# GpSimd's sums of the second weights (experts 3 to 7) in six operations of 128x384 in place of three of 128x768

## The chip, the cores and the metric

The kernel runs on one core of one Trainium2 chip. Its time is the device time of one execution in microseconds (us), lower is better. Five engines of the core take part, each with its own queue of instructions in order: PE (TensorE, the matrix products), DVE (VectorE), ACT (ScalarE), POOL (GpSimd) and SP (SyncE, which issues most DMAs). PEld is the loading of the stationary operand on PE; it overlaps the products. Everything here is float32.

## The reference, cut to what matters

An attention-like recurrence makes 3072 rows of 384 numbers. Each row then goes to the one of eight experts with the highest gate value, through two matrices of that expert with a ReLU between them:

```python
y = _attn_ref(q, k, v, f_logit)          # state = f * state + k v^T ; y = q . state
x = y.transpose(0, 2, 1, 3).reshape(B * S, H * D)     # 3072 x 384
logits = x @ w_gate                                   # 384 x 8
expert_idx = np.argmax(logits, axis=1)
...
for e in range(E):                                    # 8 experts
    h = np.maximum(x_sorted[lo:hi] @ w1[e], 0.0)      # w1: 384 x 1024
    y_sorted[lo:hi] = h @ w2[e]                       # w2: 1024 x 384
...
return gate_w[:, None] * y
```

## The kernel before, in words

The first third of the program is the recurrence, the routing and a scatter of the rows into one region of DRAM per expert. The change touches only what follows: a loop over the experts, with three tiles of 128 rows (or 352 rows, where short leftovers ride along) for each.

**The wide part of an expert** is x @ w1. It is not done as a plain product but by a fast scheme over blocks, with fewer products and more sums: `w1` is cut into 4 x 3 blocks (256 hidden columns by 128 inputs each) and the rows into halves. 17 sums and differences of the blocks of `w1`, each 128x256, are made ahead (lines 1302 to 1307, tiles `was` and `w1t`; "the first sums" from here on); DVE makes sums of the rows (`xbs`). `widen_sums` then runs 20 products on PE, two matmuls each, into five PSUM banks. Their results are put together by a table of steps, `WIDE_STEPS`: `keep` is a copy of a bank to SBUF by ACT (line 1415), `join` an addition of a bank and an SBUF tile by DVE, `more` an addition of two SBUF tiles by DVE (both line 1392), `rect` a ReLU by ACT (line 1422). A new product that needs a bank waits for the last reader of that bank. The steps that the prediction speaks of stand in this order in the table:

```
add:c31:a32:bs4 join:c31:c31:+:c10
more:c31:c31:-:c11 rect:c31:- add:t4:a30:bs6 keep:t4:h0 pass:t4:t1 ...
new:t9:as3:bs7 keep:t9:c20 pass:t9:c11 join:c11:c11:+:c01
more:c11:c11:+:c10 rect:c11:+ ... join:c01:c01:+:c00 ...
```

In ACT's queue the order is: ReLU of `c31`, then the copy `h0` (tile `hold`, which frees the bank of `t4` for the product `as5`), then the copy of `t9`. In DVE's queue: join and `more` of `c31`, two joins, `more` of `c11`, the join of `c01` (which frees a bank for the product with `a22`).

**The narrow part** is h @ w2. The last tile of 128 rows goes through a plain product (`narrow_riding` or `narrow_late`). The other two tiles go as a pair (`narrow_pair`) through a scheme with seven products of half blocks in place of eight. It needs three sums of quarters of `w2`, made by `weight_sums`: `t1`, `t2`, `t4`, each 128 x 4 x 192, which is 768 numbers per partition ("the second sums", line 1298, tiles `wsum1`, `wsum2`, `wsum4`). `t2` reads `t1`, and `t4` reads `t2`. For experts 0 to 2 DVE makes them, for experts 3 to 7 POOL.

**The order of the work** is written out by hand: each engine runs its instructions in the order of the code, under `manual_schedule`. For an expert e above 2 the code gives POOL this: the second sums of e, the first sums of e+1, the scatter of the riding tile's rows of e, the two scatters of the pair of e (line 260; the pair's two wait for DVE's `ysb`, line 1480), then the second sums of e+1, and so on. PE runs the wide part of e, the last tile, the pair of e, the wide part of e+1; between them stand short products for leftover rows (lines 1256 and 1279). So POOL begins the second sums of an expert at about the time at which PE begins that expert's wide part.

Of the kernel before, what the change touches and what calls it, by code (L numbers as in the profile page):

```python
# [170 lines left out]
def kernel(  # L171
# [15 lines left out]
    nc = tc.nc  # L187
# [189 lines left out]
    def load_rows(row, count=C):  # L377

        rows = xs[ds(row, count)] if not isinstance(row, int) else xs[row : row + count]
        n, whole = -(-count // C), count // C  # L380
        wholes = rowp.tile([128, TILES * C // BK, DB], F32, name="xrow")
        x = wholes[:, 0 : count // BK]
        tg = rowp.tile([128, TILES, USED - TOK], F32, name="tg", bufs=4)[:, 0:n]
        reads = load_blocks(x, rows)
        reads.append(
            nc.sync.dma_start(
                tg[:, 0:whole], rows[0 : whole * C, TOK:USED].rearrange("(t p) r -> p t r", p=C)
            ).ins
        )
        if n > whole:  # L390
            nc.sync.dma_start(tg[0 : count - whole * C, whole], rows[whole * C :, TOK:USED])
        return {"n": n, "rows": count, "x": x, "tg": tg, "reads": reads, "whole": wholes}
# [821 lines left out]
    with ExitStack() as st:  # L1214
# [80 lines left out]
        HB = NF // 2  # L1295

        def minus(to, a, b, on=nc.vector):
            on.tensor_tensor(to, a, b, op=OP.subtract)  # L1298
# [125 lines left out]
        def weight_sums(w, on=nc.vector, room=None):  # L1424

            b = [
                [w[1][:, HB * i : HB * i + HB, HD * j : HD * j + HD] for j in range(2)]
                for i in range(2)
            ]
            if room is None:  # L1430
                t1, t2, t4 = (qp.tile([128, HB, HD], F32, name=f"wsum{i}") for i in (1, 2, 4))
            else:
                t1, t2, t4 = (
                    room[:, 2 * i : 2 * i + 2].rearrange("p a (b d) -> p (a b) d", b=2)
                    for i in range(3)
                )
            minus(t1, b[0][1], b[0][0], on)
            minus(t2, b[1][1], t1, on)
            minus(t4, b[1][0], t2, on)
            return b, t1, t2, t4  # L1440

        def hidden_parts(x):
# [98 lines left out]

        rooms = [qp.tile([128, NF, DM], F32, name="qw2", bufs=4) for i in range(3)]
        made = {0: weight_sums(weights[0])}
        turn(rows_of[0])
        made[1] = weight_sums(weights[1], room=rooms[0])

        def tasks(e, hook):
# [24 lines left out]
        def wide_part(e):  # L1572
            x, w = rows_of[e], weights[e]
            x["wide"] = e not in PLAIN
            if e == 1:
                x["hT"] = rooms[2][:, :, 0 : x["rows"]]
            else:
                x["hT"] = qp.tile([128, NF, TILES * C], F32, name="hT")[:, :, 0 : x["rows"]]
            wide_quad(3 * e)
            tasks(e, 0)  # L1580
            fetch(3 * e)
            if e > 1:
                made[e] = weight_sums(w, nc.vector if e == 2 else nc.gpsimd)
            if e + 1 < E and e != 1:
                prepare_weights(rows_of[e + 1], weights[e + 1])
            if x["wide"]:
                widen_sums(x)
            else:
                widen(x, w, bank, range(NF))
            if e > 0:  # L1590
                nc.scalar.copy(x["dst"], x["tg"][:, :, 0])
# [31 lines left out]
        for e in range(2, E):  # L1623
            x, w = rows_of[e], weights[e]
# [24 lines left out]
    with tc.If(todo > 0):  # L1649
# [80 lines left out]
        with ExitStack() as st:  # L1730
            bank, narrow_late, psz = tile_pools(st)
            hp = st.enter_context(tc.tile_pool(name="hp", bufs=1))
            with tc.For_i(0, E) as e:
# [10 lines left out]
                with tc.For_i(e * REGION + skip, rows_to, C) as at:  # L1744
                    x = load_rows(at)
# [64 lines left out]
```

## Time and profile before

| | us |
|---|---|
| time of one execution, median of 3 runs | 358.92 (358.86 to 360.59) |
| the profiled execution, its own time | 362.03 |
| its span in the profile | 360.3 |
| PE busy / DVE busy / POOL busy in the span | 344.2 / 275.7 / 247.5 |
| POOL, second sums, 15 operations of 128x768 | 1.81 to 1.99 each |
| POOL, first sums, 128x256 | 0.72 to 1.51 each |

Times in the rows of the trace count from the start of the span. A row of the timeline gives the start, the duration, the engine, the line of the code, the operation with what it writes and reads, and in square brackets how long the engine had been idle before it and what ended that. The profiled execution took 3.1 us longer than the median of the runs, so differences are taken inside the profile and then set beside the median.

### The profile page before, as it was taken

The numbers are of one execution on the slowest core, as the hardware profiler recorded it, in microseconds if no ns is written. First come the engines' busy times: TensorE is split into PE (matmuls) and PEld (weight loads), VectorE is DVE, ScalarE is ACT, GpSimd is POOL, SyncE is SP. The second block draws the span as 40 slices with busy tenths as digits, with TensorE's granted clock in tenths as the row PEclk, the third lists the DMA queues.
The fourth block names the chain that finished last, engine by engine and source line by source line (L and its number), as shares of the span: only waits on it lengthen the run. The fifth ranks groups of instructions, "written<-read, shape, count | busy, mean of one in ns | idle before, by whom it ended". The sixth has DMA issues, their size and how long they took to land.

```text
span 360.3 us, 10263 instructions
## 1 busy us (share of the span) xinstructions
PE 344.2 (96%) x3962; PEld 295.4 (82%) x3962; DVE 275.7 (77%) x487; ACT 172.9 (48%) x372; POOL 247.5 (69%) x273
## 2 busy tenths in 40 slices
PE   8699998999999999999999999999999999999993
PEld 8488887888889868999997797896996896599682
DVE  5899989888984847489677858868978967977840
ACT  6999897876623211551443254155245234335310
POOL 6064785785875689699997499399485989935122
PEclk9799999999999999999999999999999999999998
DMA  6999879788948944999982899799179999980241
GB/s 196 359 324 351 291 256 358 262 295 315 323 130 279 366 116 116 311 291 371 391 300 64 268 387 338 216 365 376 36 183 384 226 349 389 372 305 17 70 153 47
DMA packets 57352, 94.97 MB, mean 264 GB/s; under 512 B 21016, under 2 KB 41307, under 8 KB 56272
## 3 DMA queue, kind: packets, MB, share of 16 engines
q1 hardware_dynamic: 54128, 84.60, 70.9%
q0 software_dynamic: 3168, 9.64, 7.0%
q8 instruction: 33, 0.54, 0.6%
q14 instruction: 23, 0.19, 0.2%
HBM read 79.22 MB, written 15.21 MB: 262 GB/s over the span
## 4 chain that ended last, share of the span: by engine, by line
PE 74%; DMA 8%; POOL 7%; issue 3%; ACT 3%; DVE 1%; SPq 1%; another core or an unknown queue 1%; POOLq 0%; ACTq 0%
PE hps L1404 15%; PE yps L1462 14%; PE yt L647 9%; PE tr L650 6%; PE yps L1279 6%; PE s L647 5%; DMA w2t<-in_moe_w_dram 4%; PE tr L647 4%; PE hps L436 3%; POOL was L1307 3%; PE hps L1256 2%; PE hps L1462 2%; DMA w1t<-in_moe_w_dram 2%; POOL w1t L1307 2%; POOL wsum L1298 2%
## 5 line engine op out<-in xcount | busy, mean ns | idle before, releaser
L260 POOL DMA_INDIRECT out_dram<-ysb,dst x26 | 28.5, 1096 | 48.2 <-DVE ysb L1480 22.5
L1422 ACT ACTIVATE hT<-hT 128x352 f32<-128x352 f32 (+1 forms) x48 | 23.9, 506 | 38.3 <-DVE hT L1392 38.1
L260 POOL DMA_INDIRECT xs<-xr,posi x24 | 27.4, 1140 | 19.0 <-issue 6.0
L1462 PE MATMUL yps<-w2t,hT 128*128 128x192 f32 x224 | 39.1, 328 | 0.0
L1462 PEld LDWEIGHTS yps<-w2t,hT 128*128 128x128 f32 x224 | 36.6, 190 | 3.0 <-issue 2.5
L1404 PE MATMUL hps<-xbs,w1t 128*128 128x176 f32 (+2 forms) x216 | 35.7, 309 | 0.3 <-POOL w1t L1307 0.3
L1307 POOL TENSOR_TENSOR was<-w1t 128x256 f32<-128x256 f32 x35 | 29.6, 863 | 7.4 <-DMA w1t<-in_moe_w_dram 3.8
L721 POOL TENSOR_TENSOR k<-k,r 128x512 f32<-128x512 f32 x20 | 28.3, 1424 | 8.6 <-ACT r L717 5.3
L1392 DVE TENSOR_TENSOR hT<-hps,hT 128x352 f32<-128x352 f32 (+1 forms) x42 | 22.2, 529 | 15.5 <-PE hps L1404 9.9
L1404 PEld LDWEIGHTS hps<-xbs,w1t 128*128 128x128 f32 x216 | 32.5, 190 | 0.6 <-issue 0.5
L1415 ACT COPY hT<-hps 128x352 f32<-128x352 f32 (+1 forms) x54 | 24.8, 459 | 16.7 <-PE hps L1404 4.7
L775 DVE COPY_PREDICATED at<-mpack,s 128x1024 f32<-128x1024 uint8 x24 | 31.1, 1316 | 1.6 <-PE s L647 1.5
L700 DVE TENSOR_TENSOR_SCAN sum<-g,cap 128x1032 f32<-128x1032 f32 (+2 forms) x16 | 27.7, 1754 | 3.9 <-ACT g L693 3.9
L1279 PE MATMUL yps<-qw,hqT 128*32 128x192 f32 (+1 forms) x192 | 27.5, 381 | 0.4 <-issue 0.2
L1307 POOL TENSOR_TENSOR w1t<-w1t 128x256 f32<-128x256 f32 x28 | 25.9, 925 | 0.6
L647 PE MATMUL yt<-at,v 128*48 128x128 f32 x384 | 24.3, 275 | 0.1
L647 PE MATMUL s<-q,k 64*64 64x128 f32 (+1 forms) x768 | 23.0, 261 | 0.9 <-issue 0.8
L647 PEld LDWEIGHTS s<-q,k 64*64 64x64 f32 x768 | 20.7, 141 | 3.0 <-issue 2.5
L1404 PE MATMUL hps<-xbs,was 128*128 128x176 f32 (+2 forms) x120 | 21.5, 310 | 0.5 <-ACT hold L1415 0.5
L647 PEld LDWEIGHTS yt<-at,v 128*48 128x48 f32 x384 | 20.2, 123 | 2.1 <-issue 1.2
L1279 PE MATMUL yps<-w2t,hT 128*32 128x384 f32 x192 | 21.4, 487 | 0.0
L1476 ACT ACTIVATE held<-yps,tg 128x192 f32<-128x192 f32 x24 | 10.1, 420 | 21.7 <-PE yps L1462 21.7
(187 smaller groups left out, 857.5 us busy)
## 6 DMA issues: line engine op xcount, KB each, us to landing
w1t<-in_moe_w_dram SPq DMA_DIRECT2D x8, 1536.0 KB
w2t<-in_moe_w_dram SPq DMA_DIRECT2D x8, 1536.0 KB
qw<-in_moe_w_dram SPq DMA_DIRECT2D x16, 768.0 KB
qw<-in_moe_w_dram SPq DMA_DIRECT2D x8, 1536.0 KB
q<-in_qu_dram SPq DMA_DIRECT2D x11, 512.0 KB
k<-in_ku_dram SPq DMA_DIRECT2D x11, 512.0 KB
f<-in_fu_dram SPq DMA_DIRECT2D x10, 512.0 KB
xs<-pad SPq DMA_DIRECT2D x8, 600.0 KB
```

The lines of the kernel that those rows point to most:

```text
L260: ins = nc.gpsimd.indirect_dma_start(out=dst, out_offset=bass.IndirectOffsetOnAxis(ap=idx, axis=0), in_=src, in_offset=None, bounds_check= ...
L647: done["pe"] = nc.tensor.matmul(*a, **k).ins
L700: nc.vector.tensor_tensor_scan(x["sum"][:, part].rearrange("p s c -> p (s c)"), x["g"][:, part].rearrange("p s c -> p (s c)"), cap[:, part ...
L721: ins = on.tensor_tensor(k, k, units[u]["r"][:, part], op=OP.mult).ins
L775: nc.vector.copy_predicated(all_of(x["at"][:, a]), causal, all_of(x["ps", a]))
L1279: nc.tensor.matmul(yp[r], lhsT=h[:, f, at : at + T], rhs=w[:, f, cols], start=f == order[0], stop=f == order[-1], skip_group_check=True,)
L1307: on.tensor_tensor(to, first[1], second[1], op=op)
L1392: nc.vector.tensor_tensor(place(to), one, place(other), op=op)
L1404: nc.tensor.matmul(banks[n][:, g], lhsT=lhs[:, C * g : C * g + C], rhs=rhs, start=op == "new" and g == 0, stop=True, skip_group_check=True,)
L1415: nc.scalar.copy(place(more[0]), banks[n])
L1422: nc.scalar.activation(place(n), place(n), AF.Relu, scale=scale)
L1462: nc.tensor.matmul(to, lhsT=h[:, f], rhs=w[:, f], start=start and f == 0, stop=f == HB - 1, skip_group_check=True,)
```

## The change

`weight_sums` makes each of its three sums in two pieces when POOL is to make it: blocks 0 and 1 of the four, then blocks 2 and 3. On DVE (experts 0 to 2) there is one piece as before.

```diff
-            minus(t1, b[0][1], b[0][0], on)
-            minus(t2, b[1][1], t1, on)
-            minus(t4, b[1][0], t2, on)
+            cuts = [slice(0, HB)] if on is nc.vector else [slice(f, f + 2) for f in range(0, HB, 2)]
+            for to, x, y in ((t1, b[0][1], b[0][0]), (t2, b[1][1], t1), (t4, b[1][0], t2)):
+                for c in cuts:
+                    minus(to[:, c], x[:, c], y[:, c], on)
             return b, t1, t2, t4
```

`HB` is 4 and `HD` is 192, so a piece is 128x384. The line numbers behind this place grow by one.

On POOL, at the place of expert 6, these rows stood before: the three scatters of expert 5, the second sums of expert 6 and the begin of the first sums of expert 7.

```order
L260 DMA out_dram<-ysb,dst 3072x384 [waits DMASW0_49,DVE_49]
L260 DMA out_dram<-ysb,dst 3072x384 [waits DMASW1_49,DVE_49]
L1298 TENSOR_TENSOR wsum_4048<-w2t 128x768 [waits DMAHW1_49,PE_49]
L1298 TENSOR_TENSOR wsum_4049<-w2t,wsum_4048 128x768 [waits PE_49,Pool_49]
L1298 TENSOR_TENSOR wsum_4050<-w2t,wsum_4049 128x768 [waits Pool_49]
L1307 TENSOR_TENSOR was_4054<-w1t 128x256 [waits DMAHW2_49,PE_49]
L1307 TENSOR_TENSOR w1t<-w1t 128x256 [waits Pool_49]
```

At the same place of POOL's queue the changed kernel has this:

```order
L260 DMA out_dram<-ysb,dst 3072x384 [waits DMASW0_49,DVE_49]
L260 DMA out_dram<-ysb,dst 3072x384 [waits DMASW1_49,DVE_49]
L1298 TENSOR_TENSOR wsum_4057<-w2t 128x384 [waits DMAHW1_49,PE_49]
L1298 TENSOR_TENSOR wsum_4057<-w2t 128x384
L1298 TENSOR_TENSOR wsum_4058<-w2t,wsum_4057 128x384 [waits PE_49,Pool_49]
L1298 TENSOR_TENSOR wsum_4058<-w2t,wsum_4057 128x384 [waits Pool_49]
L1298 TENSOR_TENSOR wsum_4059<-w2t,wsum_4058 128x384 [waits Pool_49] x2
L1307 TENSOR_TENSOR was_4066<-w1t 128x256 [waits DMAHW2_49,PE_49]
L1307 TENSOR_TENSOR w1t<-w1t 128x256 [waits Pool_49]
```

Nothing changed places; three rows became six. Before, the second and the third sum waited for the operation just ahead of them. Now each of the pieces three to six waits for the piece two places ahead of it.

On PE, in the pair of expert 6, the product with `t4` read before:

```order
L1462 MATMUL hps<-wsum_4050,hT 128x192 [waits DVE_49,Pool_49]
L1462 MATMUL hps<-wsum_4050,hT 128x192 x3
L1462 MATMUL yps<-wsum_4048,hsum 128x192 [waits DVE_49,Activation_49]
L1462 MATMUL yps<-wsum_4048,hsum 128x192 x3
L1462 MATMUL yps<-wsum_4049,hT 128x192 [waits DVE_49,Activation_49]
```

In the changed kernel the same place reads:

```order
L1463 MATMUL hps<-wsum_4059,hT 128x192 [waits DVE_49,Pool_49]
L1463 MATMUL hps<-wsum_4059,hT 128x192
L1463 MATMUL hps<-wsum_4059,hT 128x192 [waits Pool_49]
L1463 MATMUL hps<-wsum_4059,hT 128x192
L1463 MATMUL yps<-wsum_4057,hsum 128x192 [waits DVE_49,Activation_49]
L1463 MATMUL yps<-wsum_4057,hsum 128x192 x3
```

The third of the four matmuls waits for the second piece of `t4` by itself. The queues of DVE, ACT and SP hold the same instructions in the same order as before, with the same waits.

## The prediction
> **What bounds the kernel now.** The page comes first: its span, the busy shares and the chain of work that ended last.
>
> ```profile
> span 360.3 us, 10263 instructions
> PE 344.2 (96%) x3962; PEld 295.4 (82%) x3962; DVE 275.7 (77%) x487; ACT 172.9 (48%) x372; POOL 247.5 (69%) x273
> PE 74%; DMA 8%; POOL 7%; issue 3%; ACT 3%; DVE 1%; SPq 1%; another core or an unknown queue 1%; POOLq 0%; ACTq 0%
> ```
>
> PE is busy for 344.2 of 360.3 us. POOL has 31% to spare, so its own time does not set the end; what can change the time is a wait of PE that POOL causes. The next view is the table by stretches, one stretch for the wide part of each of experts 3 to 7, cut where PE begins and ends its 20 products.
>
> ```profile
> 205.01:218.11 13.10, 13.10 (x84) 13.10 (x81) 6.39 (x12) 7.75 (x17) 12.61 (x13) 1.00 1.03 372
> 235.18:247.38 12.20, 12.20 (x88) 12.00 (x88) 8.69 (x19) 7.46 (x17) 11.72 (x12) 1.00 1.06 391
> 261.81:273.84 12.03, 12.03 (x83) 11.83 (x81) 9.07 (x21) 6.86 (x16) 7.50 (x6) 1.00 0.83 254
> 290.91:304.21 13.30, 12.50 (x82) 11.83 (x80) 8.54 (x18) 6.87 (x16) 11.76 (x12) 1.00 1.04 365
> 321.29:333.39 12.10, 12.10 (x86) 11.90 (x88) 9.76 (x23) 6.86 (x16) 7.34 (x5) 1.00 0.14 53
> ```
>
> The numbers are the stretch, its length, and the busy time of PE, PEld, DVE, ACT and POOL; then the granted clock (1.00 in all five) and the DMA share. Expert 3 has wider rows (192 columns for 176), so 13.10 us is its normal length. Of the other four, expert 6 alone is long: 13.30 against 12.03, and PE is idle in it. That is 1.27 us, and it is all that better sharing between POOL and DVE can win in these stretches. The timeline of expert 6 shows where it comes from.
>
> ```profile
> 294.23 1.83 POOL L1298 TENSOR_TENSOR wsum<-w2t 128x768 f32<-128x768 f32 x1
> 296.14 1.81 POOL L1298 TENSOR_TENSOR wsum<-w2t,wsum 128x768 f32<-128x768 f32 x1
> 296.59 1.75 DVE L1392 TENSOR_TENSOR hT<-hT 128x352 f32<-128x352 f32 x1
> 298.03 1.97 POOL L1298 TENSOR_TENSOR wsum<-w2t,wsum 128x768 f32<-128x768 f32 x1
> 298.77 0.43 ACT L1415 COPY hold<-hps 128x352 f32<-128x352 f32 x1
> 297.93 0.64 PEld L1404 LDWEIGHTS hps<-xT,was 128*128 128x128 f32 x4
> 299.32 0.60 PEld L1404 LDWEIGHTS hps<-xbs,was 128*128 128x128 f32 x4 [0.75 <-issue]
> 300.15 0.93 DVE L1392 TENSOR_TENSOR hT<-hT 128x352 f32<-128x352 f32 x1
> 301.00 0.51 DVE L1392 TENSOR_TENSOR hT<-hps,hT 128x352 f32<-128x352 f32 x1
> 301.63 0.60 PEld L1404 LDWEIGHTS hps<-xbs,w1t 128*128 128x128 f32 x4 [0.52 <-issue]
> ```
>
> The DVE operation at 296.59 is the `more` of `c31`, which adds two SBUF tiles; call it M1. Undisturbed it takes 0.53 (the row of 240.96 below). Here it began 0.45 behind the second sum, which ran to 297.95, and ended at 298.34, 0.39 after that sum. The third sum, begun 0.31 before M1's end, ran to 300.00, some 1.65 after it. So each seems to wait for the whole of the other's operation. M1's end sets ACT's ReLU, then the copy to `hold` (298.77 to 299.20), and that frees the bank for PE at 299.32: 0.98 after M1. PE was due at 297.93 + 0.60 = 298.53. The second DVE operation of this kind, M2 (`more` of `c11`), begins at 300.15, 1.81 after M1's end; a first sum that POOL began at 299.97 cost it 0.40 more. The join at 301.00 follows, and the bank it frees lets PE go on at 301.63.
>
> **How much delay is free.** With D1 the delay of M1 and d2 that of M2, PE first loses what D1 has over 298.53 - 0.98 - (296.59 + 0.53) = 0.43. The later limit comes from expert 7, where PE never stopped.
>
> ```profile
> 326.96 0.74 DVE L1392 TENSOR_TENSOR hT<-hT 128x352 f32<-128x352 f32 x1
> 329.96 0.52 DVE L1392 TENSOR_TENSOR hT<-hps,hT 128x352 f32<-128x352 f32 x1
> 329.50 1.83 PEld L1404 LDWEIGHTS hps<-xbs,w1t 128*128 128x128 f32 x12
> ```
>
> There D1 was 0.21, and the join ended at 330.48. Its product is the third of the three in the PEld row, at 0.60 each due at 330.69, or 0.12 after the join at the earliest: 0.09 to spare. So D1 + d2 may reach 0.30. The loss of a stage is the larger of D1 - 0.43 and D1 + d2 - 0.30, or nothing. For expert 6 that gives 1.22 + 0.40 - 0.30 = 1.32 against the 1.27 seen, so the rule holds within 0.05.
>
> **The change, part by part.** No row shows a 128x384 operation of POOL. The nearest are these.
>
> ```profile
> 212.48 0.73 POOL L1307 TENSOR_TENSOR was<-w1t 128x256 f32<-128x256 f32 x1
> 213.17 0.73 POOL L1307 TENSOR_TENSOR was<-w1t 128x256 f32<-128x256 f32 x1
> 148.90 1.29 POOL L1298 TENSOR_TENSOR hT<-hT 128x512 f32<-128x512 f32 x1
> 205.10 1.83 POOL L1298 TENSOR_TENSOR wsum<-w2t 128x768 f32<-128x768 f32 x1
> 210.67 0.72 POOL L1307 TENSOR_TENSOR was<-w1t 128x256 f32<-128x256 f32 x1
> ```
>
> A piece lies between 0.73 and 1.29; a straight line from 256 to 768 gives 0.73 + 1.08/4 = 1.00, which I take. Two operations where the second need not wait for the first start 0.69 apart at 0.73 each, an overlap of 0.04; one that waits for the one just ahead starts 0.08 behind its end (294.23 + 1.83 to 296.14). The pieces wait for the piece two places ahead, which is done, so I take the overlap: 0.96 from start to start. Six last 5.8 in place of the 5.57 from 205.10 to 210.67: 0.2 us more POOL per expert. This is hidden. Expert 4's first sums end at 225.84 and PE needs them at 235.18; expert 6's begin only when a DMA lands; expert 7's end at 314.28, and PE begins at 321.29:
>
> ```profile
> 224.67 1.17 POOL L1307 TENSOR_TENSOR w1t<-w1t,was 128x256 f32<-128x256 f32 x1
> 273.67 0.73 POOL L1307 TENSOR_TENSOR was<-w1t 128x256 f32<-128x256 f32 x1 [3.77 <-DMA w1t<-in_moe_w_dram]
> 313.46 0.82 POOL L1307 TENSOR_TENSOR w1t<-w1t,was 128x256 f32<-128x256 f32 x1
> ```
>
> If that cover were gone, the whole 0.2 would be PE's. The scatters behind come 0.2 later; the pair's still wait for DVE's `ysb`. PE's new wait in the pair is for pieces made long before: in expert 3 they end at about 211, and the pair's products stand about 228 (a row further down).
>
> *Expert 6.* The third piece starts at 294.23 + 1.92 = 296.15 and ends at 297.15; M1 (296.59) falls into it and ends 0.39 later, at 297.54, so D1 = 0.42. The fourth piece, blocked meanwhile, needs 384/768 of 1.65 after that and ends at 298.38; the fifth runs from 298.34 to 299.34, the sixth from 299.30 to 300.30. M2 comes at 297.54 + 1.81 = 299.35, 0.05 behind the sixth piece. Who goes first in such a near tie is seen in two rows on either side.
>
> ```profile
> 219.36 0.72 POOL L1307 TENSOR_TENSOR w1t<-was,w1t 128x256 f32<-128x256 f32 x1
> 219.39 1.11 DVE L1392 TENSOR_TENSOR hT<-hT,hold 128x384 f32<-128x384 f32 x1
> 248.89 0.53 DVE L1392 TENSOR_TENSOR hT<-hT,hold 128x352 f32<-128x352 f32 x1
> 248.90 1.11 POOL L1307 TENSOR_TENSOR w1t<-was,w1t 128x256 f32<-128x256 f32 x1
> ```
>
> The one that starts 0.03 or 0.01 earlier keeps its plain duration, and the other is stretched. So M2 waits for the sixth piece, ends at 300.69 in place of 299.88, d2 = 0.81, and the stage loses 0.42 + 0.81 - 0.30 = 0.93 where it lost 1.27: **0.34 won**. Were M2 first, d2 = 0 and the loss 0.12: 1.15 won. [...]
>
> *Experts 5 and 7.* Their second sums begin when PE has been at the wide part for 2.3 us, and M1 comes 3.36 later.
>
> ```profile
> 264.12 1.83 POOL L1298 TENSOR_TENSOR wsum<-w2t 128x768 f32<-128x768 f32 x1
> 267.48 0.73 DVE L1392 TENSOR_TENSOR hT<-hT 128x352 f32<-128x352 f32 x1
> 323.59 1.83 POOL L1298 TENSOR_TENSOR wsum<-w2t 128x768 f32<-128x768 f32 x1
> ```
>
> Before, M1 met the last 0.35 of the second sum (D1 = 0.20 and 0.21). Now the fourth piece runs from 2.88 to 3.88 after the begin, M1 ends at 4.27 in place of 3.89, and D1 = 0.38: a loss of 0.08 in each. M2, at 6.08, comes as the sixth piece ends (5.07 to 6.07), so d2 is nothing. **0.16 lost.**
>
> *Experts 3 and 4.* There M1 comes after the sums.
>
> ```profile
> 211.25 0.57 DVE L1392 TENSOR_TENSOR hT<-hT 128x384 f32<-128x384 f32 x1
> 240.96 0.53 DVE L1392 TENSOR_TENSOR hT<-hT 128x352 f32<-128x352 f32 x1
> ```
>
> The sums began at 205.10 and, for expert 4, at PE's begin less 0.60. The pieces end 0.2 later, M1 now meets a first sum for 0.16 or not at all: under 0.30, nothing lost.
>
> **Sum.** 0.16 - 0.34 = -0.18 us on the profiled execution of 362.03 (360.3 span and 1.7 around it), whose time is 3.11 above the median of the runs. Set on the median: 358.92 - 0.18, about **358.7**. The ends of the unknown: all 1.27 won, or a piece of 1.29 or with gaps, worked out below.
>
> **The rivals.**
>
> *M2 goes first* (0.25). The tie of 0.05 in expert 6 falls the other way if a piece takes 1.03 instead of 1.00. Then 0.16 - 1.15 = -1.0: 357.9. For it: the margin is less than I know the piece's duration to. Against it: the overlap row is measured, and the length is fixed by rows on both sides.
>
> *Pieces with gaps* (0.20), the case on the slower side. If each piece starts 0.08 behind the last one's end, as the long sums did, they are 1.08 apart. M1 in experts 5 and 7 meets a fourth piece from 3.24 to 4.24: D1 = 0.74, 0.44 lost in each. Expert 6 loses 0.36 and wins 0.91. POOL falls 0.9 behind in expert 3, and its last first sums meet DVE in the pair. There DVE ends at 228.03 what PE loads at 228.31:
>
> ```profile
> 227.34 0.69 DVE L1298 TENSOR_TENSOR hT<-hsum,hT 128x512 f32<-128x512 f32 x1
> 228.31 0.19 PEld L1462 LDWEIGHTS yps<-wsum,hT 128*128 128x128 f32 x1
> ```
>
> One more blocked operation (0.6) against 0.28 to spare loses 0.3. Together 0.88 + 0.3 - 0.91 = +0.3: 359.2. It decides from a gap of about 0.06 on; for it speaks that the pieces do carry waits for POOL, against it that these are long fulfilled.
>
> *No stall to win* (0.13). The stall of expert 6 hangs on when a scatter ends, and the timed executions, 3 us shorter, may not have it, or the pieces hold DVE off as one. Then nothing or the 0.16 is left: 358.9 to 359.1.
>
> **How the numbers follow.** The forecast has 0.42. All four cases lie from 357.9 to 359.2. A measurement of this kernel can tell a change of about 0.5% (1.8 us) from none, and the three runs before spread over 1.7 us, so the range adds some 0.4 us below and 0.7 above: 357.5 to 359.9. No case reaches 1.8 us either way, since the stall is 1.27 and a slower end is priced at 0.3. What is left for that is the spread of the runs and a wait that no row shows: 0.06 for faster, 0.06 for slower, 0.88 within 0.5%.
>
> **What would show it.** In the profile after: 30 rows of 128x384 at about 1.00 us, 0.96 apart where DVE leaves them alone; M1 of expert 6 at some 0.95 in place of 1.75; M2 there at 1.3 if the forecast holds, at 0.53 if the first rival does; M1 of experts 5 and 7 at 0.91; wide parts of about 12.1, 13.0 and 12.1 us for experts 5, 6 and 7. The prediction would be wrong if the wide part of expert 6 keeps 13.3, if experts 5 or 7 pass 12.5, or if the time moves though all five wide parts stay within 0.1 us of the forecast.

## The result: slower, by about 1.5%

| | before | after |
|---|---|---|
| time of one execution, median of 4 runs each, us | 359.75 (358.86 to 362.85) | 366.14 (364.01 to 367.06) |
| the profiled execution, its own time, us | 362.03 | 364.01 |
| its span, us | 360.3 | 362.2 |
| wide parts of experts 5, 6, 7 in it, us, cut alike | 12.10, 13.37, 12.10 | 14.22, 14.30, 14.01 |

The ratio, taken over the executions in the chip's fast state and not as the quotient of the two medians, is 1.0148, with a 95% interval of 1.0115 to 1.0181: 4 to 6.5 us. The forecast was 358.7, set on the 358.92 of three executions; its range ended at 359.9. It was wrong in sign and in size.

The head of the profile page after, as it was shown of before:

```profile
span 362.2 us, 10278 instructions
PE 342.6 (95%) x3962; PEld 293.0 (81%) x3962; DVE 277.8 (77%) x487; ACT 172.8 (48%) x372; POOL 245.8 (68%) x288
PE 66%; POOL 8%; DMA 7%; DVE 5%; issue 5%; SPq 4%; ACT 3%; POOLq 0%; DVEq 0%; ACTq 0%
```

PE's busy time is smaller than before, and yet the span is longer: PE waits more. The share of DVE in the chain went from 1% to 5%. The table by stretches, with one stretch for each wide part of experts 3 to 7 and the columns as before, shows the place.

```profile
201.93:215.20 13.27, 13.27 (x85) 13.27 (x82) 6.46 (x12) 7.79 (x17) 12.93 (x16) 1.00 1.03 373
232.10:244.30 12.20, 12.20 (x88) 12.00 (x88) 8.69 (x19) 7.47 (x17) 11.88 (x15) 1.00 1.05 390
258.73:272.95 14.22, 12.65 (x86) 11.89 (x88) 11.26 (x21) 6.87 (x16) 10.39 (x12) 1.00 0.87 286
289.96:304.26 14.30, 12.57 (x86) 11.89 (x88) 8.85 (x15) 6.87 (x16) 13.54 (x16) 1.00 1.05 385
321.27:335.28 14.01, 12.46 (x86) 11.90 (x88) 11.70 (x22) 6.87 (x16) 7.47 (x8) 1.00 0.08 29
```

These stretches end with PE's last product of the 20. Three of those of before, as the prediction shows them, end 0.07 to 0.17 earlier, at 218.11, 273.84 and 304.21. Cut like those of after, experts 3, 5 and 6 of before read:

```profile
205.01:218.28 13.27, 13.27 (x85) 13.27 (x82) 6.56 (x12) 7.75 (x17) 12.78 (x14) 1.00 1.03 373
261.81:273.91 12.10, 12.10 (x86) 11.90 (x88) 9.11 (x22) 6.86 (x16) 7.57 (x6) 1.00 0.83 255
290.91:304.28 13.37, 12.57 (x86) 11.90 (x88) 8.61 (x18) 6.87 (x16) 11.83 (x12) 1.00 1.04 365
```

The stall of expert 6 stays 13.37 - 12.10 = 1.27. Experts 3 and 4 are as long after as before. Experts 5, 6 and 7 take 42.53 us together where they took 37.57: 5.0 us more. The granted clock is 1.00 in all five, so it is no matter of the clock. The span grew by 1.9 only, because this execution was 3.1 us ahead when expert 3 began (201.93 against 205.01), in a part of the program that the change leaves alone; such differences of executions are why the profile's stretches, and not its span, are set beside the timed ratio.

The groups by line name the wait. The first row is of before, the second of after; the columns are count, busy time, mean ns of one, and the idle time ahead of them with what ended it.

```profile
L1404 PE MATMUL hps<-xbs,was 128*128 128x176 f32 (+2 forms) x120 | 21.5, 310 | 0.5 <-ACT hold L1415 0.5
```

```profile
L1404 PE MATMUL hps<-xbs,was 128*128 128x176 f32 (+2 forms) x120 | 21.6, 311 | 4.7 <-ACT hold L1415 4.7
```

PE waits for the copy to `hold`, 4.7 us in all where it was 0.5. That is the place of the prediction: the copy stands behind M1. The timeline of expert 5 after, cut to POOL's first and last three pieces, M1, and PE's product that waits:

```profile
261.04 1.02 POOL L1298 TENSOR_TENSOR wsum<-w2t 128x384 f32<-128x384 f32 x1
...
263.92 0.99 POOL L1298 TENSOR_TENSOR wsum<-w2t,wsum 128x384 f32<-128x384 f32 x1
264.41 2.80 DVE L1392 TENSOR_TENSOR hT<-hT 128x352 f32<-128x352 f32 x1
264.88 0.99 POOL L1298 TENSOR_TENSOR wsum<-w2t,wsum 128x384 f32<-128x384 f32 x1
265.83 0.99 POOL L1298 TENSOR_TENSOR wsum<-w2t,wsum 128x384 f32<-128x384 f32 x1
268.22 0.39 PE L1404 MATMUL hps<-xbs,was 128*128 128x176 f32 x1 [1.57 <-ACT hold L1415]
```

The pieces are as predicted: about 1.00 us, 0.95 to 0.96 apart, six in 5.78. M1 is not. It begins at 264.41 in the fourth piece, which ends at 264.91. By the forecast it should have gone in there, ahead of the fifth. It ended at 267.21, which is 0.39 after the end of the **sixth** piece (266.82). The fifth and the sixth began after M1 and kept their plain 0.99. Experts 6 and 7 show the same: M1, the last piece, and in expert 6 the first of the first sums, which POOL begins next.

```profile
295.64 2.84 DVE L1392 TENSOR_TENSOR hT<-hT 128x352 f32<-128x352 f32 x1
297.04 0.99 POOL L1298 TENSOR_TENSOR wsum<-w2t,wsum 128x384 f32<-128x384 f32 x1
297.99 1.07 POOL L1307 TENSOR_TENSOR was<-w1t 128x256 f32<-128x256 f32 x1
...
326.95 2.79 DVE L1392 TENSOR_TENSOR hT<-hT 128x352 f32<-128x352 f32 x1
328.35 0.99 POOL L1298 TENSOR_TENSOR wsum<-w2t,wsum 128x384 f32<-128x384 f32 x1
```

M1 took 2.8 us in all three, ending 0.40 and 0.45 after the last piece of the six.

### The profile page after: what moved, and what is told of

The parts are those of the page before. It is cut to its first block, busy times and chain, and to the rows that moved or that the text cites. A ratio compares the mean times of both kernels' runs of the same rounds, so it can differ in the third digit from the quotient of the medians.

```text
span 362.2 us, 10278 instructions
## 1 busy us (share of the span) xinstructions
PE 342.6 (95%) x3962; PEld 293.0 (81%) x3962; DVE 277.8 (77%) x487; ACT 172.8 (48%) x372; POOL 245.8 (68%) x288
## 4 chain that ended last, share of the span: by engine, by line
PE 66%; POOL 8%; DMA 7%; DVE 5%; issue 5%; SPq 4%; ACT 3%; POOLq 0%; DVEq 0%; ACTq 0%
PE hps L1404 14%; PE yps L1463 13%; PE yt L647 7%; PE tr L650 5%; PE yps L1279 5%; DMA qw<-in_moe_w_dram 3%; PE tr L647 3%; PE s L436 3%; PE s L647 3%; PE yps L456 3%; PE hps L436 3%; POOL was L1307 3%; DMA f<-in_fu_dram 2%; PE hps L1256 2%; PE hps L1463 2%
## 5 line engine op out<-in xcount | busy, mean ns | idle before, releaser
L260 POOL DMA_INDIRECT xs<-xr,posi x24 | 26.2, 1093 | 19.3 <-PE tr L647 4.8
L1392 DVE TENSOR_TENSOR hT<-hT 128x352 f32<-128x352 f32 (+1 forms) x24 | 22.5, 938 | 1.2
L1404 PEld LDWEIGHTS hps<-xbs,was 128*128 128x128 f32 x120 | 18.4, 190 | 5.4 <-issue 3.6
L647 PE MATMUL s<-q,k 64*64 64x128 f32 (+1 forms) x768 | 21.7, 254 | 1.0 <-POOL k L721 0.3
L647 PEld LDWEIGHTS s<-q,k 64*64 64x64 f32 x768 | 19.5, 136 | 3.4 <-issue 1.9
```

The source lines that it names most:

```text
L260: ins = nc.gpsimd.indirect_dma_start(out=dst, out_offset=bass.IndirectOffsetOnAxis(ap=idx, axis=0), in_=src, in_offset=None, bounds_check= ...
L647: done["pe"] = nc.tensor.matmul(*a, **k).ins
L1392: nc.vector.tensor_tensor(place(to), one, place(other), op=op)
L1404: nc.tensor.matmul(banks[n][:, g], lhsT=lhs[:, C * g : C * g + C], rhs=rhs, start=op == "new" and g == 0, stop=True, skip_group_check=True,)
```

## The experiments

The trace names two differences between the runs of operations of before and after: they are cut in two, and the stops between them are gone. Before, each sum waited for the one just ahead and started 0.08 behind its end. After, each piece waits for one two places back, long done, and starts 0.03 to 0.08 *before* the end of the piece ahead. The experiments separate the two. From here on a *stop* is the 0.08 us by which an operation of POOL starts behind the end of the one just ahead, since it reads what that one wrote. All edits touch only the second sums that POOL makes. The first two and that of experts 3 and 4 are edits of the changed kernel, the others of the kernel before; where a diff shows only new lines, they stand in the place of POOL's three sums. Where the sums no longer read each other, their values for experts 3 to 7 are not those of the reference. Medians and ratios stand in the table at the end of this section.

**The same pieces, stops put back.** The loops change places, so that four of the six pieces wait for the piece just ahead.

```diff
-            for to, x, y in (...):
-                for c in cuts:
+            for c in cuts:
+                for to, x, y in (...):
                     minus(to[:, c], x[:, c], y[:, c], on)
```

> The six pieces stay 128x384, but in the order t1, t2, t4 of blocks 0 and 1, then t1, t2, t4 of blocks 2 and 3, so that four of them wait for the piece just ahead, and start some 0.08 us behind its end; only the third and the fourth follow each other without that. Theory A (DVE is shut out of a run of pieces that start before the one ahead has ended): the first more of an expert (M1) waits for one piece, two at the most, and takes under 1.6 us in place of 2.8; wide parts of experts 5, 6, 7 at 12.0 to 12.6 us in place of 14.1, 14.2, 14.0; time about 5 us below the changed kernel. Theory B (pieces of two rows of 192 shut DVE out whatever their starts): M1 at 2.8 and the time of the changed kernel, within 1.5 us.

The timeline of expert 5 in this run, POOL's fourth to sixth piece and M1:

```profile
265.31 1.00 POOL L1298 TENSOR_TENSOR wsum<-w2t 128x384 f32<-128x384 f32 x1
265.54 1.15 DVE L1392 TENSOR_TENSOR hT<-hT 128x352 f32<-128x352 f32 x1
266.39 1.17 POOL L1298 TENSOR_TENSOR wsum<-w2t,wsum 128x384 f32<-128x384 f32 x1
267.64 1.00 POOL L1298 TENSOR_TENSOR wsum<-w2t,wsum 128x384 f32<-128x384 f32 x1
```

M1 comes in the fourth piece as in the changed kernel, but ends at 266.69, 0.38 after that piece; now the fifth is stretched. The wide parts of experts 5 to 7 are 12.37, 12.10 and 12.37. The loss of the change is gone with the same number of pieces of the same size, so the cut alone is not the cause.

**Smaller pieces, still no stop.** Twelve pieces of 128x192, of which none waits for the one just ahead.

```diff
-            cuts = ... [slice(f, f + 2) for f in range(0, HB, 2)]
+            cuts = ... [slice(f, f + 1) for f in range(HB)]
```

> Twelve pieces of 128x192, one block each, contiguous in each partition, in the order of the change, none waiting for the piece just ahead. Theory A: M1 waits for the end of the twelfth piece, about 6.6 us after the first began, so M1 takes some 3.4 to 4.4 us and the wide parts of experts 5 to 7 reach 14.5 to 15.5 us; slower than the changed kernel. Theory B (it is the pattern of several rows): DVE gets in after one piece, M1 at 0.5 to 1.0 us, wide parts 12.0 to 12.2, time at or a little below the kernel before. The first sums (128x256, contiguous, many started before the one ahead ended) let DVE in after one, which speaks for B.

The table by stretches, experts 5 to 7:

```profile
257.52:272.11 14.59, 12.72 (x86) 11.90 (x88) 11.63 (x21) 6.87 (x16) 11.53 (x18) 1.00 0.89 283
289.12:304.24 15.12, 12.57 (x85) 11.90 (x88) 9.67 (x15) 6.88 (x16) 14.33 (x22) 1.00 1.05 385
321.25:335.55 14.30, 12.46 (x85) 11.90 (x88) 11.99 (x22) 6.87 (x16) 8.60 (x14) 1.00 0.08 28
```

This is worse than the change. M1 came in the seventh piece and had an end of a piece each 0.55 us at which to get in, and it got in at none of the next four. One thing does not fit a plain "until the end of the run", though. In experts 5 and 7 M1 went in before the twelfth piece, not after it. Expert 5:

```profile
263.20 3.09 DVE L1392 TENSOR_TENSOR hT<-hT 128x352 f32<-128x352 f32 x1
...
265.32 0.58 POOL L1298 TENSOR_TENSOR wsum<-w2t,wsum 128x192 f32<-128x192 f32 x1
265.87 0.86 POOL L1298 TENSOR_TENSOR wsum<-w2t,wsum 128x192 f32<-128x192 f32 x1
```

M1 ended at 266.29, 0.39 after the eleventh, and the twelfth was stretched. In expert 6 it waited for all twelve (3.67 us).

**No waits at all, contiguous operands.** The pieces of the change are two strips of 192 numbers each on some operands; here they are flat.

```diff
+                for k, to in enumerate((t1, t2, t4)):
+                    flat = to.rearrange("p f d -> p (f d)")
+                    for i in range(2):
+                        minus(flat[:, DM * i : DM * i + DM], w[1][:, 2 * k + i], w[1][:, 7 - 2 * k - i], on)
```

> Six operations of 128x384 that each read 384 contiguous numbers of two blocks of w2 and wait for none of the others; the values of the three sums for experts 3 to 7 are not those of the reference. Theory A: M1 2.8 us, wide parts 14 as in the changed kernel. Theory B (rows in the pattern): M1 0.5 to 1.4, wide parts 12.0 to 12.3. Theory C (an operation of 384 or more is long enough to shut DVE out): as A.

M1 took 2.79, 2.83 and 2.80, the wide parts 14.01, 14.28 and 14.02. The pattern of the operands and the satisfied waits that the pieces carry make no difference.

**The long operations, stops taken away.** Three operations of 128x768 as before the change, but the second and the third read nothing that POOL has just made.

```diff
+            same = on is nc.vector
+            minus(t1, b[0][1], b[0][0], on)
+            minus(t2, b[1][1], t1 if same else b[0][1], on)
+            minus(t4, b[1][0], t2 if same else b[1][1], on)
```

> Three operations of 128x768 as before, but each from blocks of w2 alone, so that none waits for the one ahead; the values of the second and third sum for experts 3 to 7 are not those of the reference. Theory A: without the gap that the waits gave, M1 waits for the end of the third operation, 5.5 us after the first began: M1 2.5 to 3.5 us and wide parts of 13.7 to 14.7 us for experts 5 to 7, near the changed kernel. If only the cut into pieces matters: as before, wide parts 12.0 for experts 5 and 7, and the time of the kernel before.

The timeline of expert 5, the second and third sum and M1:

```profile
261.75 1.84 POOL L1298 TENSOR_TENSOR wsum<-w2t 128x768 f32<-128x768 f32 x1
263.10 2.64 DVE L1392 TENSOR_TENSOR hT<-hT 128x352 f32<-128x352 f32 x1
263.52 1.83 POOL L1298 TENSOR_TENSOR wsum<-w2t 128x768 f32<-128x768 f32 x1
```

M1 came in the second sum and waited for the third as well (263.10 + 2.64 = 265.74, 0.39 after 265.35). So the kernel before, without any cutting, loses the same way once its stops are gone. Together with the first experiment this shows the cause: the **stops**, not the size.

**One stop of two.** The second sum waits for the first again, the third for nothing near.

```diff
             minus(t1, b[0][1], b[0][0], on)
             minus(t2, b[1][1], t1, on)
-            minus(t4, b[1][0], t2, on)
+            minus(t4, b[1][0], t2 if on is nc.vector else b[1][1], on)
```

> Three operations of 128x768: the second waits for the first (a gap of 0.08 us), the third waits for nothing (its values for experts 3 to 7 are not those of the reference). In experts 5 and 7 M1 comes into the second operation, about 1.5 us after the gap, and the third follows without a gap. Theory A in its plain form (an operation that starts before the one ahead has ended keeps DVE out): M1 waits for the end of the third, 2.3 to 2.6 us, wide parts 13.5 to 14. [...]

```profile
262.12 1.81 POOL L1298 TENSOR_TENSOR wsum<-w2t,wsum 128x768 f32<-128x768 f32 x1
263.33 0.99 DVE L1392 TENSOR_TENSOR hT<-hT 128x352 f32<-128x352 f32 x1
263.88 2.11 POOL L1298 TENSOR_TENSOR wsum<-w2t 128x768 f32<-128x768 f32 x1
```

These are the second and third sum of expert 5 and M1. The third began 0.05 before the end of the second (263.93), without a stop, and still DVE got in ahead of it: M1 ended 0.39 after the second, and the third was stretched to 2.11. In expert 5 M1 came 0.60 before the end of the second sum, took 0.99, and the wide part was 12.21; in expert 7 it took 0.75 and the wide part 12.10. Plain theory A expected 2.3 to 2.6 and 13.5 to 14. So a stop is not needed at the place where DVE gets in. One earlier in the run is enough.

**Where the stop stands.** Six flat pieces as in the third experiment. One of them reads the output of the piece ahead: the fourth (`k == 3`), the second (`k == 1`) or the third (`k == 2`).

```diff
                 for k, to in enumerate(outs):
-                    minus(to, w[1][:, k], w[1][:, 7 - k], on)
+                    minus(to, w[1][:, k], outs[2] if k == 3 else w[1][:, 7 - k], on)
```

> The six contiguous operations of 128x384 of the run before with one wait put in: the fourth reads what the third wrote, so it starts 0.08 us behind its end; five and six wait for nothing (values of the sums not those of the reference). M1 of experts 5 to 7 comes into the fourth, some 0.3 us after the gap. Plain A: M1 still waits for the end of the sixth, 2.6 to 2.8 us, wide parts 14. [...] If only a gap right behind the running operation lets DVE in, as plain A.

> Six contiguous operations of 128x384 with the one wait at the second; values of the sums not those of the reference. M1 of experts 5 and 7 comes into the fourth, 2.3 us after the gap, and the fourth ends 2.9 us after it. [...]

> As the run before, with the one wait at the third operation: the fourth ends 1.9 us after the gap, as second operation behind it. [...] If the count of operations without a gap decides and two are enough: M1 at 2.9, wide parts 14.

M1 took 1.00 to 1.03 us in experts 5 and 7 in all three runs, and 1.35, 0.63 and 1.33 in expert 6. DVE was let in after one piece each time. With the stop at the fourth or the third, expert 6 still took 13.12 and 13.10: M1 met the whole of a piece there, and M2 took 1.07. The rule of the free delay gives 0.83 + 0.54 - 0.30 = 1.07 and 0.80 + 0.54 - 0.30 = 1.04 over 12.10. The run with the stop ahead of the second piece, expert 5, from the second piece on:

```profile
260.94 1.00 POOL L1298 TENSOR_TENSOR wsum<-w2t,wsum 128x384 f32<-128x384 f32 x1
261.91 0.99 POOL L1298 TENSOR_TENSOR wsum<-w2t 128x384 f32<-128x384 f32 x1
262.86 1.00 POOL L1298 TENSOR_TENSOR wsum<-w2t 128x384 f32<-128x384 f32 x1
263.21 1.03 DVE L1392 TENSOR_TENSOR hT<-hT 128x352 f32<-128x352 f32 x1
263.82 1.29 POOL L1298 TENSOR_TENSOR wsum<-w2t 128x384 f32<-128x384 f32 x1
```

M1 came in the third piece behind the stop and went in at its end, 263.86, which is 2.9 us after the stop. That left two readings: the time since the last stop counts (2.9 us is still let in, 3.4 to 3.9 from the begin of a run without any stop is not), or the way in which the run begins.

**A stop ahead of the run.** Two operations of 128x16, the second reading the first, and then six flat pieces without a stop.

```diff
+                minus(outs[5][:, 0:16], w[1][:, 0, 0:16], w[1][:, 1, 0:16], on)
+                minus(outs[5][:, 16:32], outs[5][:, 0:16], w[1][:, 1, 0:16], on)
                 for k, to in enumerate(outs):
                     minus(to, w[1][:, k], w[1][:, 7 - k], on)
```

> On GpSimd the values of the second sums of experts 3 to 7 are not the reference's: six contiguous pieces of 128x384 take any blocks of w2, and none waits for another. Ahead of them stand two operations of 128x16, and the second of these waits for the first. So the run of pieces has a wait just ahead of its begin, and none inside. What decides whether M1 gets in: theory 'time without a gap': M1 is asked for some 3.1 us after the gap, in the fourth piece. In the runs with one gap it was let in up to 2.9 us after the gap, in the flat run it was kept out 3.4 us after the begin. If time (or the number of pieces, 3 let in and 4 not) decides, M1 is kept out: some 2.8 us in experts 5 and 7, wide parts of 13.9 to 14.2 us, one execution at 361 to 364 us. [...]

Expert 5: the two small operations, the first flat piece, the third to fifth, and M1.

```profile
260.39 0.24 POOL L1298 TENSOR_TENSOR wsum<-w2t 128x16 f32<-128x16 f32 x1
260.70 0.22 POOL L1298 TENSOR_TENSOR wsum<-wsum,w2t 128x16 f32<-128x16 f32 x1
260.88 1.01 POOL L1298 TENSOR_TENSOR wsum<-w2t 128x384 f32<-128x384 f32 x1
...
262.80 1.02 POOL L1298 TENSOR_TENSOR wsum<-w2t 128x384 f32<-128x384 f32 x1
263.76 1.40 DVE L1392 TENSOR_TENSOR hT<-hT 128x352 f32<-128x352 f32 x1
263.76 1.01 POOL L1298 TENSOR_TENSOR wsum<-w2t 128x384 f32<-128x384 f32 x1
264.71 1.31 POOL L1298 TENSOR_TENSOR wsum<-w2t 128x384 f32<-128x384 f32 x1
```

M1 came as the fourth piece began, waited for that one, and went in at 264.77; the fifth was stretched. That is 4.1 us after the stop and 4.4 after the run's first operation, later than the 3.9 at which the changed kernel kept M1 out. So the time since the stop does not decide. M2 of expert 6 shows it once more: it began at 295.87 in the sixth flat piece and ended at 297.21, 0.38 after that piece (296.83), which is 6.3 us after the stop of 290.5. So one stop near the begin held for all six pieces. The wide parts were 12.62, 12.71 and 12.59, where the theory of time expected 13.9 to 14.2. They are longer than the 12.25, 12.67 and 12.24 of the run with the stop at the second piece: in experts 5 and 7 M1 met nearly the whole of a piece (D1 is 0.87 and 0.85), in expert 6 M2 did (1.34). This kernel was timed once.

**The change where M1 comes late.** The pieces for experts 3 and 4 only.

```diff
-            cuts = [slice(0, HB)] if on is nc.vector else ...
+            cuts = [slice(0, HB)] if on is nc.vector or not cut else ...
...
+                made[e] = weight_sums(w, ..., cut=e < 5)
```

> The change for experts 3 and 4 alone; experts 5 to 7 keep three operations of 128x768. All theories that put the loss on M1 of experts 5 to 7: no loss, within 0.5% of the kernel before; wide parts of experts 5 and 7 12.0 to 12.1. If the loss came from the later sums on POOL or from something in the pairs: a part of the 1.5% stays, 1 to 3 us.

The wide parts of experts 5 to 7 were 12.10, 13.31 and 12.10: those of before, with expert 6's stall. The time is that of before. The 0.2 us that six pieces take more is hidden in experts 3 and 4.

**The kernel before once more**, for a second profile of it.

> The kernel before once more, for a second profile of it: whether the wide part of expert 6 is long (13.3 us) in every execution, or only where its second sums begin 3.3 us after PE. If M1 met them as in experts 5 and 7, it would be 12.0 to 12.1 there, and the time in this execution 1 to 1.3 us shorter for it.

The wide parts were 12.10, 13.24 and 12.10, and M1 of expert 6 took 1.61. The stall on which the prediction built is no accident of one profile: it stands in an execution of 357.67 us, too.

**Small pieces with stops.** The loops of the first experiment with twelve pieces of 128x192: eight of them wait for the piece just ahead.

> Twelve pieces of 128x192 in the order t1, t2, t4 of block 0, then of block 1, and so on, so that two of three wait for the one just ahead. The values are those of the reference. [...] If the number of operations alone shut DVE out, M1 near 3 us and 364 as with the twelve that do not wait.

The wide parts were 12.13, 12.13 and 12.47. Expert 6's stall is gone, expert 7 gives 0.37 back, and the six operations' 5.8 us of POOL became 8.4, hidden. In the profile this is 0.8 us better than the 37.57 of before. The ratio's interval still holds 1, so it is not shown to be faster.

All runs, in us (M1 and wide parts of experts 5, 6, 7; the median time of the run and of before in the same comparison; the ratio as in the section on the result):

| run | M1 | wide parts | time | before | ratio, 95% |
|---|---|---|---|---|---|
| the change | 2.80, 2.84, 2.79 | 14.22, 14.30, 14.01 | 366.14 | 359.75 | 1.0148 (1.0115 to 1.0181) |
| same pieces, stops back | 1.15, 0.53, 1.15 | 12.37, 12.10, 12.37 | 357.96 | 358.47 | 0.9989 (0.9954 to 1.0024) |
| twelve pieces, no stop | 3.09, 3.67, 3.08 | 14.59, 15.12, 14.30 | 364.05 | 358.47 | 1.0185 (1.0126 to 1.0245) |
| six flat pieces, no stop | 2.79, 2.83, 2.80 | 14.01, 14.28, 14.02 | 362.00 | 358.47 | 1.0140 (1.0072 to 1.0209) |
| three long, no stop | 2.64, 2.40, 2.38 | 13.86, 13.85, 13.60 | 361.39 | 358.47 | 1.0083 (1.0049 to 1.0117) |
| three long, one stop | 0.99, 1.12, 0.75 | 12.21, 12.74, 12.10 | 358.42 | 357.57 | 1.0018 (0.9980 to 1.0057) |
| six flat, stop at the 4th | 1.00, 1.35, 1.01 | 12.22, 13.12, 12.23 | 358.31 | 357.57 | 1.0023 (0.9976 to 1.0069) |
| six flat, stop at the 2nd | 1.03, 0.63, 1.03 | 12.25, 12.67, 12.24 | 356.35 | 358.11 | one run |
| six flat, stop at the 3rd | 1.02, 1.33, 1.01 | 12.24, 13.10, 12.23 | 359.53 | 358.11 | one run |
| six flat, stop ahead | 1.40, 0.67, 1.38 | 12.62, 12.71, 12.59 | 357.75 | 357.12 | one run |
| experts 3 and 4 only | 0.75, 1.70, 0.74 | 12.10, 13.31, 12.10 | 357.80 | 357.57 | 0.9981 (0.9946 to 1.0016) |
| before once more | 0.73, 1.61, 0.75 | 12.10, 13.24, 12.10 | 357.67 | 357.57 | one run |
| twelve pieces, stops | 0.53, 0.53, 0.85 | 12.13, 12.13, 12.47 | 357.21 | 358.11 | 0.9976 (0.9949 to 1.0003) |

## Why the prediction was wrong

**The step that failed** is the one for experts 5 and 7: "Now the fourth piece runs from 2.88 to 3.88 after the begin, M1 ends at 4.27 in place of 3.89". The piece and M1's arrival were right to within 0.02. But M1 ended 6.17 us after the begin of the sums in expert 5 (267.21 - 261.04), not 4.27, since it had to wait for the fifth and sixth piece too. The same assumption, that M1 waits for one operation and takes the next turn, stands in the step for expert 6.

**Where the assumption came from.** The pieces without a stop were counted in the cost step, with an overlap of 0.04, and this was taken for a matter of 0.04 us per piece only. The rows that showed DVE getting in after one operation were all of operations with a stop in their run: the long sums were 0.08 apart because each waited for the one ahead. The near ties at 219.36 and 248.89, of first sums that each started 0.08 behind the operation ahead, were read as if the one that starts first always went first. After the change M1 starts first by 0.47 and goes last. The trace of before does hold rows of DVE against a run that had not stopped, in the recurrence, which the prediction did not read:

```profile
66.99 0.97 POOL L260 DMA_INDIRECT xs<-xr,posi  x1 [0.30 <-issue]
68.11 0.84 POOL L850 TENSOR_TENSOR state<-state,kept 128x384 f32<-128x384 f32 x1
68.34 2.48 DVE L743 TENSOR_TENSOR q<-q,g 128x1024 f32<-128x1024 f32 x1
68.89 0.83 POOL L850 TENSOR_TENSOR state<-state,kept 128x384 f32<-128x384 f32 x1
```

Behind the scatter of 66.99 POOL runs on without a stop (a short copy at 67.95 stands between). DVE's product, from two SBUF tiles, takes 1.20 elsewhere (56.11). Here it begins in the operation of 68.11, which ends at 68.95, and yet it ends at 70.82, 1.10 after the end of the next one (69.72), which began 0.55 after it. Where the same product waits for one operation only, it ends 1.07 after that one (53.57 after 52.50 in the trace after). So the case could have been read off before the change; the prediction did not bound it.

**The rivals.** "No stall to win" holds the clause "or the pieces hold DVE off as one", which is what happened, but prices it at nothing to 0.16. The prediction's own rule gives another price. With M1 ending 0.39 after the sixth piece, D1 in expert 5 is 2.80 - 0.53 = 2.27, and the loss 2.27 - 0.30 = 1.97; measured were 14.22 - 12.10 = 2.12. Expert 7: 1.96 by the rule, 1.91 measured. Expert 6, with an M2 of 0.77: 2.31 + 0.24 - 0.30 = 2.25, against 14.30 - 12.10 = 2.20. So the rule of the free delay held within 0.15 far outside the place from which it was taken. Three such losses less expert 6's 1.27 are about 4.9 us: 363.8 on the median shown, against 364.0 to 367.1 timed. The clause was there and the rule was there; the one was not put into the other. "Pieces with gaps", the rival on the slower side, got it the wrong way round: gaps are what helps.

**The order of the starts.** That it decides who goes first was the author's reading of two near ties, each of one operation against one. By it M1 of expert 5 would have gone in ahead of the fifth piece, and the trace has it behind the sixth. What the traces do show is that M1, where it met an operation of POOL, ended 0.38 to 0.45 after the end of one.

**What held.** The pieces' length (about 1.00), their distance (0.95 to 0.96) and the 0.2 us more per expert, hidden (the run with experts 3 and 4 alone). The length was right although "No row shows a 128x384 operation of POOL" was not: the rows of line 850 above are such, at 0.83, with an operand of 8 numbers per partition repeated. Experts 3 and 4 lost nothing: M1 comes there after the sums. Expert 6's old stall was not there to win: the sums began 2.30 after PE's begin and not 3.32, as in the other three runs without a stop. A larger stall took its place. The text named 12.5 for experts 5 and 7 as what would prove it wrong; they took 14.22 and 14.01.

**What stays open.** Four kernels without a stop kept M1 out, and one stop, in each of the five places tried, even ahead of the run, ended this: so much is shown. What in POOL does it is not. All the runs that kept M1 out start directly behind a scatter, as the rows of the recurrence above do. A run that starts after an idle time behaved otherwise. In the trace after, POOL is idle for 1.27 us until 49.28 and then runs without a stop; DVE's product of 52.18 ends at 53.57, after the one operation that ends at 52.50, and POOL's next, begun at 52.43, is stretched from 0.21 to 1.20. A near tie goes against this: in the second profile of before, after an idle time too, the product of 53.73 was passed by an operation begun 0.06 after it. And a scatter ahead is not always enough: in the run of three long operations without a stop, DVE's sum of 175.84, begun during a scatter that ends at 176.46, ended at 176.99, ahead of the first sum that POOL had begun at 176.48. So whether the begin behind a scatter is what counts, or something else that these runs share, is not shown. Nor is it explained why twelve pieces let M1 in before the last one in experts 5 and 7.

## What to carry to other kernels

When an operation on GpSimd is cut or reordered, look at which waits between neighbours disappear, not only at the length of the pieces: a small wait on the operation just ahead may be what lets DVE's sums of two SBUF tiles have a turn (M1 of expert 5: 2.80 us in the change, 1.15 with the same pieces and the stops back). In this kernel one such dependence in a run of GpSimd's operations was enough, so try to keep one in every run that lies beside work of DVE on the path, for instance by running a chain of sums block by block. And before a row is taken as proof of who goes first, see that it has the same waits around it as the case it is to stand for; each clause of a rival is to be put through the same price rule as the forecast.

## What the runs showed of the hardware

- In four kernels a run of POOL's operations that began directly behind a scatter and had no stop kept M1, DVE's sum of two SBUF tiles, out: it took 2.38 to 3.67 us (up to 3.14 over its plain 0.53), over up to three 1.0 us pieces or some six of 0.58. The operations it waited for kept their plain duration meanwhile (0.99 for the fifth and sixth piece of the change).
- One stop of 0.08 us, up to 4.1 us earlier (6.3 for M2), changed that to a wait for one operation and a little: in the rows shown M1 then ends 0.38 to 0.39 after it.
- Without a stop an operation of POOL started 0.03 to 0.08 before the end of the one ahead, in pieces from 128x192 to 128x768; the amount did not tell who is let in (0.05 in the run with one stop of two, 0.03 to 0.06 in the changed kernel's expert 5).
- An operation that had to wait for the other engine showed this as a longer duration, not as a later start: POOL's third sum in the run with one stop of two began at 263.88, before M1's end at 264.32, and took 2.11 in place of 1.83. So its start in these traces does not say that it has got its turn.
